# Attention and mixture of experts on one core: the tail rows' values as five wide float32 products, and four mixes moved ahead of five quarter operations

## The chip, the cores and the metric

The kernel runs on one core of a Trainium2 chip. The metric is the device time of one execution in microseconds (us), as the median of the runs shown. TensorE (PE) multiplies, VectorE (DVE), ScalarE (ACT) and GpSimd (POOL) work on tiles, and SyncE (SP) issues nearly all DMAs. Each engine takes its own instructions strictly in order and waits for the others by semaphores.

## The reference, cut to what matters

```python
def _attn_ref(q, k, v):                      # 2 x 8 heads x 576 rows x 64
    q_rot, k_rot = rotate(q), rotate(k)      # rotary embedding
    scores = scale * np.matmul(q_rot, k_rot.transpose(0, 1, 3, 2))
    scores = scores - np.max(scores, axis=-1, keepdims=True)
    attn = np.exp(scores)
    attn = attn / (np.sum(attn, axis=-1, keepdims=True) + 1e-09)
    return np.matmul(attn, v)

def _moe_ref(x, domain_probs, w1, w2):       # 1152 x 512, 4 experts, 1024 hidden
    p = domain_probs / (domain_probs.sum(-1, keepdims=True) + 1e-09)
    for e in range(E):
        h = np.maximum(x @ w1[e], 0.0)
        out += p[:, e:e + 1] * (h @ w2[e])

x = attn_out.transpose(0, 2, 1, 3).reshape(B * S, H * D)
return _moe_ref(x, **moe)
```

## The kernel before

**Attention.** Eight `Pair` objects, four head pairs for each of two batches, named 0_0 to 0_3 and 1_0 to 1_3. The 576 rows of a head are four row tiles of 128 and a tail of 64. A pair so has nine units: four row tiles of each head, and unit 8 (`TAIL`), which holds both heads' tails in one tile of 128 rows. For each unit TensorE makes the scores (`scores`), VectorE their maximum (`max`), ScalarE the exponentials and their row sum into column `u` of `total` (`exp`), TensorE turns the exponentials (`turn_e`, `turn_x`), and ScalarE and VectorE copy them out of PSUM in a high and a low part (`high`, `low`, `high_x`, `low_x`). Two units together make a product with V (`values`), whose two halves ScalarE and VectorE add (`lower`, `add`). These main rows are divided at the end: VectorE takes the reciprocals of `total` (`inverse`), spreads them (`spread`), TensorE turns them (`rows`), and VectorE multiplies (`divide`).

**The tail unit** goes another way. `scale` (L385) multiplies its exponentials by the reciprocals before `turn_e` turns them; `copy_e` and `copy_x` put the turned block into the tile `at` in float32; `tail_values` (L412) makes ten float32 products of 64 x 64, five for each head; `tail_high` and `tail_low` split the result, the second on VectorE.

**The order.** `Pair.place` (L432) puts every step at a due time in an agenda, from the tables `ALONE` (pairs of batch 0) and `BESIDE` (batch 1), and the program is emitted in that order. So each engine's queue is fixed by the tables. Rotations of later pairs run on GpSimd as jobs in between.

**The experts.** Rows are cut in chunk 0 (512 rows, class `Moe`) and chunk 1 (640 rows, class `Moe1`). Chunk 0 runs interleaved with the pairs of batch 1; its second layer's last results are weighted by `mix` (L605), one call per 128 rows. Chunk 1's first layer uses seven products of quarter matrices instead of eight. Sums of quarters of its input are made by `Quarters` (L624), three of four groups on GpSimd and the last, `second(nc.vector, 1)`, on VectorE. Its eight VectorE operations are `whole` and two `less`, `whole` and `less`, and three `low`. The sums of quarters of the weights are made by `Weights.sum` (L507), on GpSimd for the first block of the first expert and on VectorE for the others.

**PSUM.** The values' products of batch 0 share one bank, `xb[1]`, named x_113 before and x_114 after, in columns 256 to 511; the turned columns of keys 512 to 575 lie in `xb[0]`. From the end of batch 0 on only `xb[0]` is left for both.

```python
po = self.po = banks["x"].pick()[:, 2 * P : 2 * P + ST]
for j in range(2):
    for c in range(NS):
        n = P if c < NR else ST
        nc.tensor.matmul(po[j * D : (j + 1) * D, :], lhsT=self.raw["v"][0:n, j, c, :],
                         rhs=self.at[0:n, c, j * ST : (j + 1) * ST], start=(c == 0), stop=(c == NR))
```

Of the kernel before, what the change touches and what calls it, by code (L numbers as in the profile page):

```python
# [26 lines left out]
    copy_x=2.409, inverse=0.587, scale=0.712, spread=3.143, rows=4.075, divide=4.404, out_high=8.561,  # L27
    out_low=9.259, tail_values=4.354, tail_high=4.658, tail_low=4.771,
# [4 lines left out]
    tail_turn_x=1.122, copy_x=1.44, inverse=0.243, scale=0.697, spread=0.555, rows=2.195, divide=2.503,  # L33
    out_high=9.813, out_low=10.683, tail_values=2.033, tail_high=2.528, tail_low=2.554,
# [21 lines left out]
def kernel(  # L56
# [17 lines left out]
    nc = tc.nc  # L74
# [70 lines left out]
    class Pair:  # L145
# [9 lines left out]
        def load(self, s, queue=nc.sync, heads=((0, 2),)):  # L155

            hp, nm = self.hp, self.nm
            src = {"k": k, "q": q, "v": v}[s]
            x = self.pool.tile([P, 2, NS, D], F32, tag=f"raw{s}", name=f"raw{s}{nm}")
            hs = src[self.b, 2 * hp : 2 * hp + 2]  # L160
            for i, (a, z) in enumerate(heads):
                queue.dma_start(
                    out=x[:, a:z, 0:NR, :], in_=hs[a:z, 0:SM, :].rearrange("h (p r) d -> p h r d", r=NR)
                )
                if i:
                    continue
                for j in range(2):
                    rows = slice(j * ST, (j + 1) * ST)
                    if s == "v":
                        queue.dma_start(out=x[rows, :, NR, :], in_=hs[:, SM:S, :].rearrange("h p d -> p h d"))  # L170
                    else:
                        queue.dma_start(out=x[rows, 0, NR, :], in_=hs[j, SM:S, :])
# [29 lines left out]
        def split_v(self, eng_h=nc.gpsimd, eng_l=nc.gpsimd):  # L202
            self.vs = self.pool.tile([P, 2, NS, 2, D], F32R, tag="vs", name=f"vs{self.nm}")
            split(eng_h, eng_l, self.raw["v"], self.vs[:, :, :, 0, :], self.vs[:, :, :, 1, :])
# [105 lines left out]
        def turn_e(self, u):  # L310
# [6 lines left out]
            if u == TAIL:  # L317
                self.at = apool.tile([P, NS, P], F32, tag="at", name=f"at{nm}")
# [31 lines left out]
        def copy_e(self):  # L350
            nc.scalar.activation(out=self.at[:, 0:NR, :], in_=self.et.pop(TAIL), func=AF.Copy)

        def copy_x(self):
            nc.vector.tensor_copy(self.at[0:ST, NR, :], px[:, 0:P])
# [46 lines left out]

        def divide(self):
# [5 lines left out]
        def out_low(self):  # L408
            eng = nc.vector if (self.b, self.hp) == (B - 1, NP - 1) else nc.gpsimd
            eng.tensor_tensor(out=self.dst[1], in0=self.xf, in1=f32(self.dst[0]), op=ALU.subtract)  # L410

        def tail_values(self):  # L412
            po = self.po = banks["x"].pick()[:, 2 * P : 2 * P + ST]
            for j in range(2):
                for c in range(NS):
                    n = P if c < NR else ST
                    nc.tensor.matmul(  # L417
                        po[j * D : (j + 1) * D, :],
                        lhsT=self.raw["v"][0:n, j, c, :],
                        rhs=self.at[0:n, c, j * ST : (j + 1) * ST],  # L420
                        start=(c == 0),
                        stop=(c == NR),
                    )

        def tail_high(self):
            nc.scalar.activation(out=self.tail_dst[0], in_=self.po, func=AF.Copy)

        def tail_low(self):
            cH, cL = self.tail_dst
            nc.vector.tensor_tensor(out=cL, in0=self.po, in1=f32(cH), op=ALU.subtract)  # L430

        def place(self, u, t, step, o):  # L432
# [8 lines left out]
            if u == TAIL:  # L441
                at("tail_turn", self.turn_e, u)
                at("tail_turn_x", self.turn_x, u)
                for key in (
                    "copy_e", "copy_x", "inverse", "scale", "spread", "rows", "divide", "out_high", "out_low",
                    "tail_values", "tail_high", "tail_low",
# [676 lines left out]
```

## Time and profile before

| what | us |
|---|---|
| median of 3 runs | 574.27 |
| lowest and highest run | 572.32, 576.47 |
| the profiled execution, its own time | 573.63 |
| span of that execution, first to last instruction | 571.8 |

So 1.8 us lie around the span. The profile shows one execution. A matmul's duration there is its latency, and matmuls overlap: the pace of a row of them is the distance between their starts, or the time until the next instruction's start divided by their number. "PEld" is TensorE's weight load, which runs beside the matmuls. A row of a float32 product counts two instructions, so the ten products of a tail are "x20". The number in brackets is how long the engine had stood idle before the row, with the instruction that ended the wait.

### The profile page before, as it was taken

How to read it: one execution, taken by the hardware profiler on the slowest of the kernel's cores; microseconds unless marked ns; L12 is line 12 of the kernel's file. 1: busy time of each engine (PE TensorE's matmuls, PEld its weight loads, DVE VectorE, ACT ScalarE, POOL GpSimd, SP SyncE). 2: the span in 40 equal slices, each digit the busy share in tenths (PEclk: the TensorE clock that was granted, in tenths of full speed). 3: DMA queues.
4: the chain of work that ended last, by engine and by line, in shares of the span. 5: the costliest groups of instructions: out<-in, count | busy, mean ns of one | idle time of the engine just before them, and what ended most of it. 6: DMA issues, size and time to landing. Idle time of an engine off the chain costs nothing.

```text
span 571.8 us, 8611 instructions
## 1 busy us (share of the span) xinstructions
PE 545.8 (95%) x3229; PEld 478.5 (84%) x3229; DVE 325.4 (57%) x586; ACT 277.8 (49%) x545; POOL 337.5 (59%) x232
## 2 busy tenths in 40 slices
PE   4898988999999999999999998999999999999996
PEld 3788877888888888888888886998899899889985
DVE  5588898234362434444334435995578658757702
ACT  5678888365444544556436552554154225324500
POOL 7999965458824673379244388458663664565400
PEclk9999999899999999999999999999999999999999
DMA  5245023054224222442242222631323213223102
GB/s 151 70 115 136 18 56 97 18 172 153 73 62 156 73 75 54 121 120 70 76 104 79 66 75 76 222 107 38 109 78 100 65 57 111 75 73 78 72 0 92
DMA packets 42459, 50.67 MB, mean 89 GB/s; under 512 B 7218, under 2 KB 32050, under 8 KB 42418
## 3 DMA queue, kind: packets, MB, share of 16 engines
q1 hardware_dynamic: 41618, 49.38, 29.1%
q10 hardware_dynamic: 800, 0.75, 0.5%
q8 instruction: 25, 0.41, 0.3%
q14 instruction: 16, 0.13, 0.1%
HBM read 43.34 MB, written 2.36 MB: 80 GB/s over the span
## 4 chain that ended last, share of the span: by engine, by line
PE 78%; DVE 7%; ACT 7%; POOL 4%; issue 2%; DMA 1%; SPq 0%; ACTq 0%; POOLq 0%; DVEq 0%
PE po L824 6%; PE po L822 6%; PE po L823 6%; PE p L737 6%; PE p L739 5%; PE p L738 5%; PE sc L282 5%; PE ph L601 4%; PE ph L603 4%; PE ph L602 4%; PE po L578 4%; PE po L576 4%; PE po L577 4%; PE pp L315 4%; ACT e L301 3%; PE x L417 3%
## 5 line engine op out<-in xcount | busy, mean ns | idle before, releaser
L142 POOL TENSOR_TENSOR wl<-wr,wh 128x1024 fp32r<-128x1024 f32 x64 | 154.3, 2412 | 145.6 <-ACT wh L135 144.1
L135 ACT ACTIVATE wh<-wr 128x1024 fp32r<-128x1024 f32 x64 | 67.2, 1052 | 28.8 <-PE po L578 16.7
L293 DVE TENSOR_REDUCE mx<-sc 128x1 f32<-128x576 f32 x72 | 54.2, 752 | 37.7 <-PE sc L282 37.3
L301 ACT ACTIVATE e<-sc,mx 128x576 f32<-128x576 f32 x72 | 53.3, 740 | 22.1 <-DVE mx L293 21.6
L142 POOL TENSOR_TENSOR sl<-sf,sh 128x1024 fp32r<-128x1024 f32 x16 | 38.5, 2404 | 42.5 <-ACT sh L135 42.5
L824 PE MATMUL po<-wh,hL 128*128 128x512 f32 x160 | 62.3, 389 | 0.0
L823 PE MATMUL po<-wl,hH 128*128 128x512 f32 x160 | 62.3, 389 | 0.0
L822 PE MATMUL po<-wh,hH 128*128 128x512 f32 x160 | 62.3, 389 | 0.0
L562 DVE SCALAR_TENSOR_TENSOR hL<-ph,hH 128x512 fp32r<-128x512 f32 x32 | 22.1, 692 | 61.1 <-ACT hH L561 61.1
L576 PE MATMUL po<-wh,hH 128*128 128x512 f32 x128 | 52.3, 409 | 0.0
L601 PE MATMUL ph<-xH,wh 128*128 128x512 f32 x128 | 51.5, 402 | 0.0
L315 PE MATMUL pp<-ident,e 128*128 128x128 f32 x288 | 45.3, 281 | 5.9 <-DVE e L387 3.4
L332 ACT ACTIVATE ptH<-pp 128x512 fp32r<-128x512 f32 x64 | 38.1, 595 | 25.1 <-PE x L365 17.3
L578 PE MATMUL po<-wh,hL 128*128 128x512 f32 x128 | 50.3, 393 | 0.0
L336 DVE TENSOR_TENSOR ptL<-pp,ptH 128x512 fp32r<-128x512 f32 x64 | 43.9, 686 | 11.1 <-ACT ptH L332 10.8
L603 PE MATMUL ph<-xH,wl 128*128 128x512 f32 x128 | 50.1, 392 | 0.0
L577 PE MATMUL po<-wl,hH 128*128 128x512 f32 x128 | 50.0, 391 | 0.0
L602 PE MATMUL ph<-xL,wh 128*128 128x512 f32 x128 | 50.0, 391 | 0.0
L135 ACT ACTIVATE sh<-sf 128x1024 fp32r<-128x1024 f32 x16 | 16.9, 1059 | 67.1 <-DVE sf L516 67.1
L775 ACT ACTIVATE hH<-p 128x320 fp32r<-128x320 f32 x64 | 27.1, 435 | 40.3 <-DVE p L767 40.3
L315 PEld LDWEIGHTS pp<-ident,e 128*128 128x128 f32 x288 | 34.3, 143 | 12.2 <-issue 2.0
L516 DVE TENSOR_TENSOR sf<-wr 128x256 f32<-128x256 f32 x30 | 32.2, 1114 | 17.4 <-DMA wr<-in_moe_w_dram 17.4
(164 smaller groups left out, 1375.3 us busy)
## 6 DMA issues: line engine op xcount, KB each, us to landing
wr<-in_moe_w_dram SPq DMA_DIRECT2D x68, 512.0 KB, 3.6
k2T<-kT SPq DMA_DIRECT2D x14, 288.0 KB, 4.1
rawv<-in_v_dram SPq DMA_DIRECT2D x8, 256.0 KB, 3.1
out_dram<-acc SPq DMA_DIRECT2D x8, 256.0 KB, 2.5
rawk<-in_k_dram SPq DMA_DIRECT2D x7, 256.0 KB, 4.1
rawq<-in_q_dram SPq DMA_DIRECT2D x7, 256.0 KB, 3.0
rawv<-in_v_dram SPq DMA_DIRECT2D x16, 32.0 KB, 2.6
tabs<-in_rope_dram ACTq DMA_DIRECT2D x1, 320.0 KB, 3.5
```

Source lines behind the costliest of these rows:

```text
L135: nc.scalar.activation(out=hi, in_=src, func=AF.Copy)
L142: eng_l.tensor_tensor(out=lo, in0=src, in1=f32(hi), op=ALU.subtract)
L315: nc.tensor.transpose(pp[:, c * P : (c + 1) * P], self.e[u][:, c * P : (c + 1) * P], ident)
L576: nc.tensor.matmul(po[t], lhsT=sH, rhs=wH, start=(f == 0), stop=False)
L577: nc.tensor.matmul(po[t], lhsT=sH, rhs=wL, start=False, stop=False)
L578: nc.tensor.matmul(po[t], lhsT=sL, rhs=wH, start=False, stop=(f == NF - 1))
L601: nc.tensor.matmul(o, lhsT=wH[:, kt], rhs=xh, start=(kt == 0), stop=False)
L602: nc.tensor.matmul(o, lhsT=wH[:, kt], rhs=xl, start=False, stop=False)
L603: nc.tensor.matmul(o, lhsT=wL[:, kt], rhs=xh, start=False, stop=(kt == KT1 - 1))
L822: nc.tensor.matmul(po[t], lhsT=sH, rhs=wH, start=(f == 0), stop=False)
L823: nc.tensor.matmul(po[t], lhsT=sH, rhs=wL, start=False, stop=False)
L824: nc.tensor.matmul(po[t], lhsT=sL, rhs=wH, start=False, stop=(f == NF - 1))
```

## The change

- `scale` is gone. The exponentials of the tail are turned as they are.
- The transposed tail products have the reciprocals along the free axis. `tail_rows` turns `total`'s last column, broadcast to 128 columns, into 128 columns of PSUM; `keep_tail_rows` copies two blocks of 64 x 64 of them into the tile `xt` on ScalarE; `tail_divide` multiplies the two blocks of the product by them on VectorE.
- `tail_values` makes five products of 128 x 128: both heads' V side by side times all 128 tail columns. Only the two blocks of equal head are used. For that raw V is laid out with the heads inside, so its load is two DMAs of one head each, in rows of 256 bytes.
- The last 64 keys go into a constant tile `tail_keys`, whose lower half is set to zero at the start.
- `tail_low` reads `xt` and runs on GpSimd, except for the last pair.
- The swapped K of the very first pair (`lh`) takes the place of another tile.
- At the end of chunk 0, the four mixes now stand ahead of five of the eight quarter operations on VectorE.

```diff
 ALONE = dict(
-    copy_x=2.409, inverse=0.587, scale=0.712, spread=3.143, rows=4.075, divide=4.404, out_high=8.561,
+    out_low=9.259, tail_rows=1.6, keep_tail_rows=2.405, tail_values=4.354, tail_divide=4.658, tail_high=4.659, tail_low=4.771,
...
+            if s == "v":
+                x = self.pool.tile([P, NS, 2, D], F32, tag="rawv", name=f"rawv{nm}")
+                for j in range(2):
+                    queue.dma_start(out=x[:, 0:NR, j, :], in_=hs[j, 0:SM, :].rearrange("(p r) d -> p r d", r=NR))
+                for j in range(2):
+                    rows = slice(j * ST, (j + 1) * ST)
+                    queue.dma_start(out=x[rows, NR], in_=hs[:, SM:S, :].rearrange("h p d -> p h d"))
...
-            self.lh = apool.tile([P, NS, P], F32R, tag="at", name=f"lh{self.nm}")
+            self.lh = odds.tile([P, NS, P], F32R, tag="vs", name=f"lh{self.nm}")
...
-            nc.vector.tensor_copy(self.at[0:ST, NR, :], px[:, 0:P])
+            nc.vector.tensor_copy(tail_keys[0:ST], px[:, 0:P])
...
-        def scale(self):
-            e = self.e[TAIL]
-            nc.vector.tensor_scalar_mul(e, e, self.total[:, TAIL:])
...
+        def tail_rows(self):
+            self.prt = xb[1][:, 0:P] if banks["x"].n > 1 else xb[0][:, 3 * P : 4 * P]
+            nc.tensor.transpose(self.prt, self.total[:, TAIL:].to_broadcast([P, P]), ident)
+
+        def keep_tail_rows(self):
+            self.xt = apool.tile([P, ST], F32, tag="xt", name=f"xt{self.nm}", bufs=2)
+            for rows, cols in self.blocks():
+                nc.scalar.activation(out=self.xt[rows], in_=self.prt[rows, cols], func=AF.Copy)
+
+        def blocks(self):
+            return [(slice(j * D, (j + 1) * D), slice(j * ST, (j + 1) * ST)) for j in range(2)]
...
         def tail_values(self):
-            ...
+            po = self.po = banks["x"].pick()[:, 2 * P : 3 * P]
+            for c in range(NS):
+                nc.tensor.matmul(
+                    po,
+                    lhsT=self.raw["v"][:, c].rearrange("p h d -> p (h d)"),
+                    rhs=self.at[:, c, :] if c < NR else tail_keys,
+                    start=(c == 0),
+                    stop=(c == NR),
+                )
+
+        def tail_divide(self):
+            for rows, cols in self.blocks():
+                nc.vector.tensor_tensor(
+                    out=self.xt[rows], in0=self.po[rows, cols], in1=self.xt[rows], op=ALU.mult
+                )
 
         def tail_high(self):
-            nc.scalar.activation(out=self.tail_dst[0], in_=self.po, func=AF.Copy)
+            nc.scalar.activation(out=self.tail_dst[0], in_=self.xt, func=AF.Copy)
 
         def tail_low(self):
             cH, cL = self.tail_dst
-            nc.vector.tensor_tensor(out=cL, in0=self.po, in1=f32(cH), op=ALU.subtract)
+            self.spare_engine().tensor_tensor(out=cL, in0=self.xt, in1=f32(cH), op=ALU.subtract)
...
-    for x in qTt:
+    for x in (*qTt, tail_keys):
         nc.gpsimd.memset(f32(x), 0.0)
...
-    for i in range(6):
-        plan.at(end + last - 1.3 + 0.01 * i, quarter_step)
+    plan.at(end + last - 1.3, quarter_step)
...
         for x in moe0[0].mixes:
             moe0[0].mix(*x)
+        for _ in range(5):
+            quarter_step()
```

TensorE's queue at the tail of the first pair. `pp_0_8` is its turned tail, `sc_1_1` are scores of the next pair. Before:

```order
L315 MATMUL pp_0_8_544<-ident,e_0_8_513 128x128 x4
L282 MATMUL sc_1_1_565<-kT_1_415,qT_1_500 128x288 x2
L282 MATMUL sc_1_1_565<-k2T_1_427,qT_1_500 128x288 x2
L341 MATMUL x_112<-ident,e_0_8_513 64x128
L315 MATMUL pp_1_0_575<-ident,e_1_0_561 128x128 x4
```

And now:

```order
L322 MATMUL pp_0_8_547<-ident,e_0_8_517 128x128 x4
L407 MATMUL x_114<-ident,total_0_244 128x128
L289 MATMUL sc_1_1_569<-kT_1_419,qT_1_504 128x288 x2
L289 MATMUL sc_1_1_569<-k2T_1_431,qT_1_504 128x288 x2
L348 MATMUL x_113<-ident,e_0_8_517 64x128
L322 MATMUL pp_1_0_579<-ident,e_1_0_564 128x128 x4
```

The new row `x_114<-ident,total` stands between the turned tail and the next pair's scores, and it writes the bank that holds the values of the pair's third product.

ScalarE's queue at the same place, now (before, `at` was followed by `e_1_1` directly):

```order
L379 ACTIVATE tmp_0_2_557<-x_114 64x256
L308 ACTIVATE e_1_0_564,total_1_521<-sc_1_0_522,mx_1_0_553 128x576
L358 ACTIVATE at_0_8_552<-pp_0_8_547 128x512
L412 ACTIVATE xt_0_587<-x_114 64x64 x2
L308 ACTIVATE e_1_1_592,total_1_521<-sc_1_1_569,mx_1_1_577 128x576
```

The two copies into `xt` stand ahead of the exponentials of the next pair's second unit.

VectorE's queue at the end of chunk 0. `s` and `tL` are quarter operations, `acc` the mixes, `sf_1` weight sums of chunk 1. Before:

```order
L410 TENSOR_TENSOR xL_76<-xf_3_3536,xH_74 128x512
L644 TENSOR_TENSOR s_3926<-xH_74,xL_76 128x320
L649 TENSOR_TENSOR s_3863<-s_3926,s_3863 128x320
L649 TENSOR_TENSOR s_3926<-s_3926,s_3865 128x320
L644 TENSOR_TENSOR s_3932<-xH_74,xL_76 128x320
L649 TENSOR_TENSOR s_3932<-s_3932,s_3926 128x320
L660 TENSOR_TENSOR tL<-s_3863,tH 128x320
L660 TENSOR_TENSOR tL<-s_3926,tH 128x320
L660 TENSOR_TENSOR tL<-s_3932,tH 128x320
L611 SCALAR_TENSOR_TENSOR acc_0_1510<-po_3_0_3672,probs,acc_0_1510 128x512
L611 SCALAR_TENSOR_TENSOR acc_1_1511<-po_3_1_3673,probs,acc_1_1511 128x512
```

And now:

```order
L666 TENSOR_TENSOR s_3936<-xH_74,xL_76 128x320
L671 TENSOR_TENSOR s_3872<-s_3936,s_3872 128x320
L671 TENSOR_TENSOR s_3936<-s_3936,s_3874 128x320
L633 SCALAR_TENSOR_TENSOR acc_0_1517<-po_3_0_3682,probs,acc_0_1517 128x512
L633 SCALAR_TENSOR_TENSOR acc_1_1518<-po_3_1_3683,probs,acc_1_1518 128x512
L633 SCALAR_TENSOR_TENSOR acc_2_1519<-po_3_2_3684,probs,acc_2_1519 128x512
L633 SCALAR_TENSOR_TENSOR acc_3_1520<-po_3_3_3685,probs,acc_3_1520 128x512
L666 TENSOR_TENSOR s_3986<-xH_74,xL_76 128x320
L671 TENSOR_TENSOR s_3986<-s_3986,s_3936 128x320
L682 TENSOR_TENSOR tL<-s_3872,tH 128x320
L682 TENSOR_TENSOR tL<-s_3936,tH 128x320
L682 TENSOR_TENSOR tL<-s_3986,tH 128x320
```

The mixes have passed the last two sums and three `tL`; the same twelve operations stand ahead of `sf_1` in both.

## Rows read from the trace of the kernel before

**Rows 1.** The page, busy time of each engine in the span.

```profile
PE 545.8 (95%) x3229; PEld 478.5 (84%) x3229; DVE 325.4 (57%) x586; ACT 277.8 (49%) x545; POOL 337.5 (59%) x232
```

**Rows 2.** Windows: stretch, length, busy time of each engine (instructions), granted clock, DMA share, GB/s.

```profile
60.00:80.00 20.00, 18.19 (x153) 16.37 (x152) 16.91 (x30) 16.60 (x43) 19.26 (x18) 1.00 0.19 47
100.40:103.90 3.50, 3.50 (x22) 2.93 (x20) 1.16 (x3) 0.38 (x1) 0.00 (x0) 0.51 0.00 0
220.00:280.00 60.00, 60.00 (x348) 51.31 (x347) 25.63 (x44) 30.84 (x57) 33.65 (x22) 1.00 0.31 87
```

**Rows 3.** Waits: engine, line, what for: us in total, times, longest.

```profile
PE pp L315 <- DVE e L387: 3.4, 3, 1.8
PE p L737 <- DVE acc L611: 0.8, 1, 0.8
```

**Rows 4.** Lines: group, count, busy us, mean ns of one, idle before.

```profile
L315 PE MATMUL pp<-ident,e 128*128 128x128 f32 x288 | 45.3, 281 | 5.9 <-DVE e L387 3.4 <-DVE ptL L336 1.5 <-ACT e L301 0.9
L315 PEld LDWEIGHTS pp<-ident,e 128*128 128x128 f32 x288 | 34.3, 143 | 12.2 <-issue 2.0 <-ACT e L301 1.8 <-ACT tmp L372 1.6
L417 PE MATMUL x<-at,rawv 128*64 128x64 f32 (+1 forms) x160 | 15.0, 237 | 0.0
L387 DVE TENSOR_SCALAR e<-e,total 128x576 f32<-128x576 f32 x8 | 6.3, 788 | 0.1
L430 DVE TENSOR_TENSOR xL<-x,xH 128x64 fp32r<-128x64 f32 x8 | 1.8, 222 | 2.8 <-ACT xH L426 2.8
```

**Rows 5.** Timeline of the first pair's tail: start us, us, engine, line.

```profile
35.49 0.38 ACT L372 ACTIVATE tmp<-x 64x256 f32<-64x256 f32 x1 [0.22 <-PE x L368]
35.65 0.51 PE L282 MATMUL sc<-kT,qT 128*128 128x288 f32 x2
41.23 1.80 PE L417 MATMUL x<-at,rawv 128*64 128x64 f32 x20
42.95 0.66 PE L315 MATMUL pp<-ident,e 128*128 128x128 f32 x4
```

**Rows 6.** Timeline of the tail of pair 0_3, up to its tail products.

```profile
96.97 1.43 DVE L387 TENSOR_SCALAR e<-e,total 128x576 f32<-128x576 f32 x1
98.55 0.63 PE L315 MATMUL pp<-ident,e 128*128 128x128 f32 x4 [1.40 <-DVE e L387]
...
99.38 0.41 DVE L376 TENSOR_TENSOR xf<-x,tmp 64x256 f32<-64x256 f32 x1
...
99.84 0.39 PE L365 MATMUL x<-ptH,vs 128*128 128x256 f32 x1
...
102.42 2.38 PE L417 MATMUL x<-at,rawv 128*64 128x64 f32 x20
```

**Rows 7.** Timeline from the tail of pair 1_3 into chunk 1.

```profile
347.27 0.63 PE L315 MATMUL pp<-ident,e 128*128 128x128 f32 x4 [1.83 <-DVE e L387]
...
354.50 1.21 DVE L410 TENSOR_TENSOR xL<-xf,xH 128x512 fp32r<-128x512 f32 x1 [0.56 <-ACT xH L406]
...
358.47 1.03 DVE L644 TENSOR_TENSOR s<-xH,xL 128x320 f32<-128x320 f32 x1
...
361.14 2.72 DVE L611 SCALAR_TENSOR_TENSOR acc<-po,probs,acc 128x512 f32<-128x512 f32 x4
...
363.92 0.41 PE L737 MATMUL p<-xH,wh 128*128 128x320 f32 x1 [0.83 <-DVE acc L611]
...
376.18 0.48 DVE L777 SCALAR_TENSOR_TENSOR hL<-p,hH 128x320 fp32r<-128x320 f32 x1
...
377.21 0.31 PE L737 MATMUL p<-t1H,sh 128*128 128x320 f32 x1
```

**Rows 8.** The page's DMA issues: KB each, median us from issue to landing.

```profile
rawv<-in_v_dram SPq DMA_DIRECT2D x8, 256.0 KB, 3.1
...
rawv<-in_v_dram SPq DMA_DIRECT2D x16, 32.0 KB, 2.6
```

**Rows 9.** Timeline, the first reader of a loaded V.

```profile
10.52 0.77 ACT L135 ACTIVATE vs<-rawv 128x640 fp32r<-128x640 f32 x1
```

More of the change, by code (lines that the diff above doesn't have):

```diff
@@ L26 @@
     low_x=2.545, values=3.917, lower=4.47, add=4.785, tail_turn=1.096, copy_e=1.588, tail_turn_x=2.02,
-    copy_x=2.409, inverse=0.587, scale=0.712, spread=3.143, rows=4.075, divide=4.404, out_high=8.561,
-    out_low=9.259, tail_values=4.354, tail_high=4.658, tail_low=4.771,
+    copy_x=2.409, inverse=0.587, spread=3.143, rows=4.075, divide=4.404, out_high=8.561,
+    out_low=9.259, tail_rows=1.6, keep_tail_rows=2.405, tail_values=4.354, tail_divide=4.658, tail_high=4.659, tail_low=4.771,
 )
@@ L32 @@
     low_x=1.378, values=2.085, lower=2.576, add=2.643, tail_turn=1.093, copy_e=1.225,
-    tail_turn_x=1.122, copy_x=1.44, inverse=0.243, scale=0.697, spread=0.555, rows=2.195, divide=2.503,
-    out_high=9.813, out_low=10.683, tail_values=2.033, tail_high=2.528, tail_low=2.554,
+    tail_turn_x=1.122, copy_x=1.44, inverse=0.243, spread=0.555, rows=2.195, divide=2.503,
+    out_high=9.813, out_low=10.683, tail_rows=2.032, keep_tail_rows=2.1, tail_values=2.033, tail_divide=2.527, tail_high=2.528,
+    tail_low=2.554,
 )
@@ L167, in load @@
                 for j in range(2):
[L168 to L172, printed above, removed]
+                    queue.dma_start(out=x[j * ST : (j + 1) * ST, 0, NR, :], in_=hs[j, SM:S, :])
             self.raw[s] = x
@@ L350, in copy_e @@
         def copy_e(self):
[L351 removed]
+            nc.scalar.activation(out=self.at, in_=self.et.pop(TAIL), func=AF.Copy)
         def copy_x(self):
[L354 removed]
+            nc.vector.tensor_copy(tail_keys[0:ST], px[:, 0:P])
         def values(self, g):
@@ L408, in out_low, with spare_engine @@
         def out_low(self):
-            eng = nc.vector if (self.b, self.hp) == (B - 1, NP - 1) else nc.gpsimd
-            eng.tensor_tensor(out=self.dst[1], in0=self.xf, in1=f32(self.dst[0]), op=ALU.subtract)
+            self.spare_engine().tensor_tensor(out=self.dst[1], in0=self.xf, in1=f32(self.dst[0]), op=ALU.subtract)
         def tail_values(self):
[L413 to L423, printed above, removed]
+            po = self.po = banks["x"].pick()[:, 2 * P : 3 * P]
[12 more added lines that the diff above has]
+                )
         def tail_high(self):
-            nc.scalar.activation(out=self.tail_dst[0], in_=self.po, func=AF.Copy)
+            nc.scalar.activation(out=self.tail_dst[0], in_=self.xt, func=AF.Copy)
         def tail_low(self):
             cH, cL = self.tail_dst
-            nc.vector.tensor_tensor(out=cL, in0=self.po, in1=f32(cH), op=ALU.subtract)
+            self.spare_engine().tensor_tensor(out=cL, in0=self.xt, in1=f32(cH), op=ALU.subtract)
+        def spare_engine(self):
+            return nc.vector if (self.b, self.hp) == (B - 1, NP - 1) else nc.gpsimd
         def place(self, u, t, step, o):
@@ L444, in place @@
                 for key in (
-                    "copy_e", "copy_x", "inverse", "scale", "spread", "rows", "divide", "out_high", "out_low",
-                    "tail_values", "tail_high", "tail_low",
+                    "copy_e", "copy_x", "inverse", "spread", "rows", "divide", "out_high", "out_low", "tail_rows", "keep_tail_rows",
+                    "tail_values", "tail_divide", "tail_high", "tail_low",
                 ):
@@ L876 @@
     apool = attn.enter_context(tc.tile_pool(name="apool", bufs=1, side="right"))
+    tail_keys = apool.tile([P, P], F32, name="tail_keys")
     evens, odds = pools("pair")
```

9 lines of the change are left out of this document (6 added, 3 removed).

## The prediction

> **What bounds the kernel now.** Read the page's busy times first: PE is busy 545.8 of 571.8 us, the next engine, GpSimd, 337.5 [rows 1]. So 26 us of the span are not PE's, and a change pays in only two ways: by less work on PE, or by fewer of its waits. Then the windows, to see where PE is full. In 60 us of batch 1 it is busy for 60.00 [rows 2], so whatever leaves its queue there comes off the time at once. The list of waits tells which idle time the change can reach: 3.4 us in three waits of the turned tail for `scale` on DVE, and one wait of 0.83 us of chunk 1's products for the last mix [rows 3, 7]. The groups by line give prices: the tail products take 160 rows in all, 20 in each pair [rows 4]. Timelines come last, at the places where the order was changed.
>
> One line in the windows does not look like waiting, but is. From 100.40 to 103.90 PE is never idle, yet its granted clock is 0.51, the lower level of 1.2 GHz, where the stretches beside it have 1.00 [rows 2]. It follows the tail of pair 0_3, where PE had stood 1.40 us for `scale` [rows 6].
>
> **The tail products.** Before, 20 PE instructions of 64 columns go from 41.23 to the next start at 42.95: 1.72 us, or 0.086 each [rows 5]. Now there are 10 of 128 columns and one transpose of 128 columns. No such product is in the trace, so its price is bounded. The low end is the pace of the narrow ones, 0.086: the columns cost nothing. The high end takes the weight load as not hidden, 0.143 for a 128 x 128 float32 load [rows 4] in front of those 0.086: 0.23. The nearest row is the float32 transpose of 128 columns. Four of them span 0.63 us with the last one's latency, which is 0.281 in the mean, so (0.63 − 0.281) / 3 = 0.116 [rows 4, 6]. The latencies say something close: 281 ns at 128 columns less 237 at 64 is 0.044, and 0.086 + 0.044 = 0.13 [rows 4]. I take 0.115, since the transposes run at that pace with loads of the same size. Then a pair costs 10 x 0.115 + 0.115 = 1.27 instead of 1.72, which saves 0.46, or **3.7 us** in eight pairs. At the low end the gain is 8 x (1.72 − 0.98) = 6.0; at the high end there is a loss of 8 x (2.42 − 1.72) = 5.5. All eight pairs count in full, because PE is full around seven of them, and in pair 0_3 the products stand directly before the first expert's.
>
> **The waits for `scale`.** In pair 1_3 PE stands 1.83 us for it [rows 7]. The turned tail needs no division now, its exponentials are long there, and PE's next work is ready: **1.8 us**. In pair 0_3 the wait of 1.40 goes as well, but something else comes next. The third product's values started at 99.84, after the sum `xf` on DVE (99.38 + 0.41 = 99.79), because both use one bank [rows 6]. With the 1.43 us of `scale` out of DVE's queue, that sum ends about 1.4 earlier, at 98.4. But then the two copies into `xt`, which read the new columns in that bank, have to leave ScalarE first: 64 x 64 each, priced below the 0.38 that the 64 x 256 copy takes [rows 5], at about 0.25. That gives 99.0 as the new start, and a gain of **0.84**. In the third place the wait was 3.4 − 1.83 − 1.40 = 0.2, in pair 0_2. There I count **0.4**, that wait and as much again, since DVE's queue is shorter ahead of the values too. This is the least certain of the small terms.
>
> **The slow stretch.** 3.5 us at 0.51 do what would take about 1.75 at full clock [rows 2]. The tail products alone take 2.38 there against 1.80 [rows 5, 6]. The clock fell some 0.6 us behind the two stalls of that tail. The larger is removed and a stall of perhaps 0.8 us stays in front of the values, so the fall is more likely gone than not: **1.7 us**, else nothing.
>
> **The new handovers.** `tail_rows` writes the bank that ScalarE's `tmp` is still reading, so it cannot start before that copy ends. In the first pair the copy ends at 35.49 + 0.38 = 35.87, while the next pair's scores, which stand behind `tail_rows` in PE's queue, started at 35.65 [rows 5]. So about 0.2 is lost there, and as much or less in pair 0_1: **−0.3** in all. Behind the waiting transpose stand those scores, and behind them their maximum on DVE; neither has much slack this early. In batch 1 the transpose waits for the same sum `xf` that the products waited for before, and everything after it is on other engines: nothing.
>
> **What is hidden.** The copies into `xt` (under 0.8 us a pair on ScalarE, which is busy 49%), the zeroing of `tail_keys`, the new place of `lh` and `tail_low` on GpSimd cost nothing. GpSimd has 0.74 us left in 20 at its fullest [rows 2], but the waits show none of PE's for GpSimd behind the first stretch of the kernel; without that cover a `tail_low` of some 0.3 us would show in full. On DVE two `tail_divide`, each nearest to the 0.22 of `xL` [rows 4], replace one `scale` and one `tail_low`, so DVE becomes lighter in every pair but not at the one place where it is tight (below).
>
> V's load moves the same 256 KB in rows of 256 bytes and two DMAs. The tails' loads already go in such rows, and land in 2.6 us against 3.1 for the large one [rows 8]. The first V, issued at about 4.2, is read only at 10.52 [rows 9], so even a doubled landing of 6.2 would end near then: 0 by the rows, 0.4 at the worst.
>
> The Trainium skill, "DMA: Bandwidth & Descriptors", section Specifications, speaks against this edit: below 512 bytes a transfer does not reach line rate, because it turns into a read and a write-back. By it the time would come to 565.8 instead of 565.4. The trace's one case of such rows, the tails' load, is too small to show it either way.
>
> **The end of chunk 0.** The five quarter operations that the mixes pass took from 358.47 to 361.14, 2.67 us, so PE's wait of 0.83 for the last mix is gone [rows 7]. It is not free. The same twelve operations stand ahead of the weight sums, and for the last pair `tail_divide` and `tail_low` sit on DVE ahead of them, about +0.5 for the chain through `xL` at 354.50. DVE is then nearly the bound in chunk 1: the `hL` that ends at 376.18 + 0.48 = 376.66 frees a bank that PE wants at 377.21 [rows 7], a margin of 0.55. PE comes 0.83 earlier and DVE 0.5 later, so PE waits about 0.8 there. What the stall returns is taken again: **0**, with 0.8 to either side.
>
> **The sum.** 3.7 + 1.8 + 0.84 + 0.4 + 1.7 − 0.3 + 0 = 8.2. Against the profiled execution's 573.63, which is 571.8 of span and 1.8 around it, that is **565.4 us**. The median of the runs shown is 0.6 above that execution; the runs differ by more among themselves (572.3 to 576.5), so I add nothing.
>
> **Rivals.** *The slow stretch stays:* a stall of about 0.8 is left just before it, and the clock did fall behind stalls of 1.40 and 0.33. Against it, the stall is shorter. Without the 1.7: 567.1. *The wide products are no faster:* if the pace follows the columns fully, an instruction takes 0.172 and the products stay at 1.72, with the transpose on top. The first term turns from +3.7 to −0.9, and the time is 570.0. The transposes' 0.116 at 128 columns speaks against it. *DVE's backlog in chunk 1 is larger:* `tail_divide` has to wait for PE's product and ScalarE's copy, and each weight sum that comes late delays products. A loss of 1.5 gives 566.9. *Slower than before:* the loads of both heads' V are not hidden behind products of 128 columns, and an instruction costs 0.23. The products lose 5.5; of the 4.5 us of all other terms 2.8 stay, with the slow stretch kept: 573.63 + 5.5 − 2.8 = 576.3. It decides from the point where 8 x (10 w + 0.115 − 1.72) exceeds 2.8, at w = 0.196 us an instruction. PE's 0.086 with 64-column products, whose loads are hidden, speaks against it.
>
> **How the numbers follow.** Forecast 0.48, slow stretch 0.22, wide products no faster 0.15, backlog 0.10, slower 0.05. The range has its low end where the products reach 0.095 (8 x (1.72 − 1.06) = 5.3, or 1.6 more) and the boundary gives its 0.8 plus a little: 562.5. Its high end takes in the rival with no faster products, 570.0, with some of its small terms missed: 571.5. About 1%, 5.7 us here, is what a measurement of this kernel can tell from no change, so "faster" means below 568.5. Nearly all of the forecast (0.46), two thirds of the slow stretch's case (0.14) and some of the others (0.07) lie below: 0.67. Slower by over 1% needs more than the last rival's 576.3, so it has 0.03. The rest, 0.30, is within 1%.
>
> **What would show it.** In the changed profile the products should read "x10" with about 1.2 us from their start to the next instruction's; 1.7 or more makes the first term wrong. The waits for `scale` should be gone, with none over 0.4 of `tail_rows` for `tmp` or of the values for `xt` in batch 0. The window behind pair 0_3's tail should show a clock of 1.00, and PE's wait at the start of chunk 1 should turn up some 13 us later, as one for `hL`, or nowhere. The forecast is wrong if PE's busy time falls by less than 2 us, or if new waits of PE on DVE or ScalarE add up to more than 2 us.

## The result and the profile after

| | before | changed | ratio, 95% interval |
|---|---|---|---|
| first comparison, median | 573.62 us (4 runs) | 567.47 us (4 runs) | 0.9886 (0.9851 to 0.9921) |
| second comparison, median | 573.78 us (11 runs) | 567.71 us (6 runs) | 0.9903 (0.9877 to 0.9928) |
| the profiled execution | 573.63 us, span 571.8 | 566.62 us, span 564.8 | |

The change saves about 6 us, 1.0 to 1.1%, where 8.2 were forecast. The ten runs of the changed kernel lie between 566.4 and 569.6, so the profiled one is among the fastest; a second profile of it, from the second comparison, is of one of the slowest (569.33, span 567.5).

The lines below are from the first of the two. The busy times of the changed kernel's page answer to [rows 1]:

```profile
span 564.8 us, 8507 instructions
PE 539.7 (96%) x3157; PEld 474.3 (84%) x3157; DVE 324.0 (57%) x587; ACT 281.0 (50%) x561; POOL 339.3 (60%) x240
```

PE's busy time fell by 6.1 us, nearly all of the 7.0 by which the span fell. So its idle time hardly changed, 25.1 us after 26.0. The list of PE's waits says why (engine, line, what for: total, times, longest):

```profile
PE p L759 <- DVE hL L799: 1.3, 2, 0.8
...
PE sc L289 <- ACT kT L243: 0.7, 2, 0.4
...
PE x L372 <- ACT xt L412: 0.6, 1, 0.6
PE ph L624 <- POOL xL L424: 0.4, 1, 0.4
PE p L759 <- ACT p L766: 0.3, 1, 0.3
```

The 3.4 us for `scale` and the 0.8 for the last mix of [rows 3] are gone. In their place stand these, none of which the list of before has. Four of the five are for VectorE or ScalarE, 2.9 us together.

The tail of pair 0_3 on PE answers to [rows 6] (start, us, engine, line):

```profile
96.56 0.39 PE L372 MATMUL x<-ptH,vs 128*128 128x256 f32 x1 [0.57 <-ACT xt L412]
...
98.16 1.06 PE L430 MATMUL x<-at,rawv 128*128 128x128 f32 x8
99.05 0.39 PE L430 MATMUL x<-tail_keys,rawv 128*128 128x128 f32 x2
99.20 0.48 PE L623 MATMUL ph<-xH,wh 128*128 128x512 f32 x1
...
102.20 0.50 PE L624 MATMUL ph<-xL,wh 128*128 128x512 f32 x1 [0.43 <-POOL xL L424]
```

Ten wide products take 1.04 us (98.16 to 99.20). The start of chunk 1 answers to [rows 7]; PE first, from two stretches of its timeline, then VectorE:

```profile
364.38 0.42 PE L759 MATMUL p<-t1H,sh 128*128 128x320 f32 x1 [0.49 <-DVE hL L799]
369.84 0.41 PE L759 MATMUL p<-t1H,sh 128*128 128x320 f32 x1 [0.78 <-DVE hL L799]
```

```profile
345.36 1.27 DVE L449 TENSOR_TENSOR xL<-xt,xH 128x64 fp32r<-128x64 f32 x1 [0.32 <-ACT xH L445]
346.55 1.38 DVE L424 TENSOR_TENSOR xL<-xf,xH 128x512 fp32r<-128x512 f32 x1
...
350.81 2.73 DVE L633 SCALAR_TENSOR_TENSOR acc<-po,probs,acc 128x512 f32<-128x512 f32 x4
353.45 1.83 DVE L666 TENSOR_TENSOR s<-xH,xL 128x320 f32<-128x320 f32 x1
...
369.30 0.48 DVE L799 SCALAR_TENSOR_TENSOR hL<-p,hH 128x320 fp32r<-128x320 f32 x1
```

**Where the time went.** Take one PE instruction that both profiles have, and compare its start. The last column is what was gained since the row above it.

| PE instruction | before | after | difference | this stretch |
|---|---|---|---|---|
| turned last columns before the tail of 0_3 | 91.67 | 89.17 | −2.50 | −2.50: the tails of 0_0 to 0_2 |
| first value of the third product of 0_3 | 99.84 | 96.56 | −3.28 | −0.78: the wait of 1.40, less new waits |
| first product of the first expert | 104.74 | 99.20 | −5.54 | −2.26: products and slow stretch |
| fourth product that reads an `xL` there, the first of pair 0_3 | 107.16 | 102.20 | −4.96 | +0.58: wait for `xL` |
| `rows` of pair 1_2 | 291.81 | 285.05 | −6.76 | −1.80: three tails of batch 1 |
| turned tail of pair 1_3 | 347.27 | 338.46 | −8.81 | −2.05: the wait of 1.83 |
| `rows` of pair 1_3 | 352.42 | 342.99 | −9.43 | −0.62: its products |
| chunk 1, first product behind the mixes | 363.92 | 353.59 | −10.33 | −0.90: the wait for the mix |
| chunk 1, product of `t1H` of the second group | 377.21 | 369.84 | −7.37 | +2.96: waits for VectorE |
| the end of the span | 571.8 | 564.8 | −7.0 | +0.37 |

Up to 353.59 the gain has grown to 10.3 us; the forecast's terms add up to 9.0 there. Then 2.96 us are handed back within 16 us.

The second profile has the same table within 0.05 us in every stretch, but for two: the first is −0.25 instead of −2.50, and that of the tails of batch 1 is −1.30 instead of −1.80. Its end is 4.3 us ahead of before. Four kernels of the experiments have the same program as the changed one up to the first of these instructions, and start it at 90.47, 91.17, 91.24 and 91.45; the old program with the new order starts it at 91.15. So the −2.50 of the table is not shown to be the change's: five of six profiles of the new program lie at 90.47 or later, and the two of the old at 91.15 and 91.67.

### The profile page after: what moved, and what is told of

It reads as the page before. It is cut to its first block, busy times and chain, and to the rows that moved or that the text cites. A ratio compares the mean times of both kernels' runs of the same rounds, so it can differ in the third digit from the quotient of the medians.

```text
span 564.8 us, 8507 instructions
## 1 busy us (share of the span) xinstructions
PE 539.7 (96%) x3157; PEld 474.3 (84%) x3157; DVE 324.0 (57%) x587; ACT 281.0 (50%) x561; POOL 339.3 (60%) x240
## 5 line engine op out<-in xcount | busy, mean ns | idle before, releaser
L343 DVE TENSOR_TENSOR ptL<-pp,ptH 128x512 fp32r<-128x512 f32 x64 | 44.0, 687 | 11.1 <-ACT ptH L339 10.3
```

## The experiments

All times are medians, and the ratios are to the kernel before, run beside each kernel. The changed kernel stands at 0.9886 and 0.9903 in its two comparisons.

**1. The order of the mixes, apart from the tails.** Once the changed kernel with the old order, once the kernel before with the new one:

```diff
-    plan.at(end + last - 1.3, quarter_step)
+    for i in range(6):
+        plan.at(end + last - 1.3 + 0.01 * i, quarter_step)
...
-        for _ in range(5):
-            quarter_step()
```

> The changed kernel with the eight quarter operations ahead of the four mixes, as before the change. Theory (the mixes' place only moves a wait: VectorE has the same queue up to the first hL of chunk 1): TensorE waits 2.5 to 3.5 us for the last mix at the start of chunk 1, and in return its waits for hL (1.3 us in the changed kernel) and the 0.5 us of other small waits there vanish; 0 to 1 us slower than the changed kernel, 567.5 to 568.5. Rival (the new order itself made VectorE late): the waits for hL vanish and the wait for the mix is under 1.5 us, 1 to 3 us faster than the changed kernel, 564.5 to 566.5. Second rival (the order is worth the stall it removes and more): 2 to 3 us slower, 569.5 to 570.5.

> The kernel before with the four mixes ahead of five of the eight quarter operations, nothing else changed. Theory: the wait of 0.83 us for the last mix goes, and since TensorE then stands only 0.83 us earlier against VectorE, with a margin of 0.55 us at hL, about 0.3 us comes back as a wait for hL: 0.5 us faster than before, 572.5 to 573.5. Rival (the order costs by itself): waits for hL of over 1.5 us, 1 us slower, 574.5 to 575.

With the new order alone: 574.0 us, ratio 1.000 (0.9986 to 1.0014). Its waits for the mixes are gone, and PE waits for something else (list of waits):

```profile
PE p L737 <- DVE hL L777: 1.2, 2, 0.8
```

So the theory's mechanism holds, the wait moves on, but all of it came back: PE's product of `t1H` of the second group starts at 377.19, and at 377.21 in the kernel before. The rival, that the order costs by itself, is right in part. VectorE's rows say where, with GpSimd's last:

```profile
354.07 1.21 DVE L410 TENSOR_TENSOR xL<-xf,xH 128x512 fp32r<-128x512 f32 x1 [0.56 <-ACT xH L406]
...
360.67 1.97 DVE L644 TENSOR_TENSOR s<-xH,xL 128x320 f32<-128x320 f32 x1
...
364.29 0.75 DVE L516 TENSOR_TENSOR sf<-wr 128x256 f32<-128x256 f32 x2
```

```profile
359.88 2.42 POOL L142 TENSOR_TENSOR sl<-sf,sh 128x1024 fp32r<-128x1024 f32 x1 [1.17 <-ACT sh L135]
```

The sum that the mixes passed took 1.03 us at its old place [rows 7] and takes 1.97 here, beside GpSimd's `sl`. From `xL` to the first weight sum VectorE needs 10.22 us; before it needed 9.28, to the row

```profile
363.78 0.78 DVE L516 TENSOR_TENSOR sf<-wr 128x256 f32<-128x256 f32 x2
```

So the new order by itself makes VectorE 0.94 us later.

With the tails alone: 570.3 us, 0.9927 (0.9899 to 0.9955), some 1.4 to 2.4 us behind the changed kernel, though the intervals overlap. That is more than the theory's 0 to 1; the time itself is one that the second rival gave. In its profile the waits for `hL` are gone, and these stand there instead:

```profile
356.56 0.41 PE L759 MATMUL p<-xH,wh 128*128 128x320 f32 x1 [1.70 <-DVE acc L633]
358.53 0.64 PE L759 MATMUL p<-xH,wh 128*128 128x320 f32 x1 [0.83 <-DVE acc L633]
```

That is 2.5 us, as the theory had it. What it did not have is the clock behind them (window: length, busy PE, PEld, DVE, ACT, POOL, granted clock, DMA share, GB/s):

```profile
358.00:364.00 6.00, 5.47 (x20) 5.47 (x21) 4.45 (x11) 2.14 (x4) 2.78 (x2) 0.50 0.60 226
```

PE's lag behind the changed kernel grows from 4.9 us at the second wait to 7.1 at 363.2, at the lower level, 1.2 GHz. (2.3 of the lag were there before the waits, from the first stretch of the table.) Two of the eight runs took 567.0 and 567.4 us, as long as the changed kernel.

The granted clock of every run, in the mean over its span, is on record. With the tails alone it is 0.988 to 0.995 in the eight runs, 0.992 in the mean, and 0.995 and 0.993 in the two short ones; in the ten runs of the changed kernel it is 0.993 to 1.000, 0.998 in the mean. An estimate from these means: what the lower level costs, at half speed, is (1 − clock) x span, 4.5 us with the tails alone and 1.3 in the changed kernel. The 3.2 between them are more than the whole loss. So the order is worth nothing by itself, and the 1.4 to 2.4 us that it seems to be worth behind the new tails go with the clock. That the two waits bring it down was not tried.

**2. Narrow products, and V's load.** Ten products of 64 x 64 on the new layout, then these with V loaded by one DMA as before:

```diff
...
+            for j, (rows, cols) in enumerate(self.blocks()):
...
+                    nc.tensor.matmul(
+                        po[rows, cols],
+                        lhsT=self.raw["v"][0:n, c, j, :],
+                        rhs=self.at[0:n, c, cols] if c < NR else tail_keys[0:n, cols],
...
```

```diff
-                x = self.pool.tile([P, NS, 2, D], F32, tag="rawv", name=f"rawv{nm}")
+                x = self.pool.tile([P, 2, NS, D], F32, tag="rawv", name=f"rawv{nm}")
...
+                queue.dma_start(
+                    out=x[:, :, 0:NR, :], in_=hs[:, 0:SM, :].rearrange("h (p r) d -> p h r d", r=NR)
+                )
...
```

> The changed kernel with ten products of 64 x 64 a pair again, on the same layout of V, the division still behind them. Theory (TensorE bound; ten instructions of 128 columns take 1.04 us and twenty of 64 take 1.72): 8 x 0.68 = 5.4 us more TensorE time, of which up to 1.2 may vanish where a later wait swallows it (pairs 0_0, 0_1 and the last pair, behind which VectorE is late): 4.2 to 5.4 us slower than the changed kernel, 571.7 to 572.9. Rival (the width pays little, the rest of the change made the gain): under 2 us slower, below 569.5.

> The kernel with narrow products, with V laid out and loaded as before the change: one DMA in rows of 1 KB in place of two in rows of 256 bytes. Theory (the load is hidden in either form): the time of the narrow kernel, 571.4, within 0.5 us; the large load lands in about 3.1 us, no engine waits for V in either. Rival (a load in rows of 256 bytes comes late or slows others): 0.5 us or more faster than the narrow kernel, below 570.9, and the first split of V begins earlier.

Narrow: 571.38 us, 0.9966 (0.9950 to 0.9983), so the width is worth 0.6 to 0.8%, 3.6 to 4.6 us, around the theory's low end of 4.2. In batch 1 PE falls behind the changed kernel by 0.60, 0.76, 0.76 and 0.76 us at the four tails. The rival with under 2 us falls. With one load: 571.78, 0.9963 (0.9946 to 0.9981), no difference. The pages give the landing (KB each, median us), changed kernel first, then the one load:

```profile
rawv<-in_v_dram SPq DMA_DIRECT2D x16, 128.0 KB, 3.0
```

```profile
rawv<-in_v_dram SPq DMA_DIRECT2D x8, 256.0 KB, 2.8
```

Half the bytes in 256-byte rows land no sooner than the whole in rows of 1 KB, so such rows may well be slower per byte. But the first reader of V starts at 11.06 with one load and at 10.99 with two: the load is hidden in either form.

**3. The wait for `scale`, put back.**

```diff
+        def scale(self):
+            e = self.e[TAIL]
+            nc.vector.tensor_scalar_mul(e, e, 1.0)
...
```

The tables give it its old due times again.

> The changed kernel with the scale operation back at its old due times, multiplying the tail's exponentials by 1.0, so that the turned tail waits for it again. Theory: the waits of the turned tail for it come back with 1.8, 1.4 and 0.2 us, and some 0.5 us of other waits: 3.4 to 4.5 us slower than the changed kernel, 571 to 572; the stretch behind the tail of pair 0_3 shows the granted clock at 0.5 again and costs 1.7 us of this or on top of it. Rival (VectorE, late at the start of chunk 1, swallows the wait of pair 1_3): 1.5 to 2 us slower, 569 to 569.5. For the clock: if it does not fall behind a stall of 1.4 us there, the fall before was not that stall's.

572.4 us, 0.9978 (0.9961 to 0.9995): 0.75 to 0.92% or 4.3 to 5.3 us slower than the changed kernel, at or above the theory's end. The two long waits are back:

```profile
98.33 0.63 PE L322 MATMUL pp<-ident,e 128*128 128x128 f32 x4 [1.40 <-DVE e L407]
...
344.18 0.63 PE L322 MATMUL pp<-ident,e 128*128 128x128 f32 x4 [1.83 <-DVE e L407]
```

Against the changed kernel PE loses 1.58 and 1.99 us at them; 0.27 of the first is won back at the next products, and 1.0 of the second at the start of chunk 1. That leaves 2.3 us, in a traced run of 571.15. The rest is in part the clock: its mean is 0.992 to 0.997 in the ten runs, 0.995 in the mean, which by the estimate of experiment 1 costs about 1.6 us more than in the changed kernel. But it does not fall where the theory said: behind the wait of 1.40 us the clock stayed up (window as above):

```profile
98.00:104.00 6.00, 4.88 (x34) 4.30 (x35) 3.60 (x10) 1.81 (x6) 0.06 (x1) 1.00 0.01 3
```

**4. The new handovers.** First the other PSUM bank, then a later place:

```diff
-            self.prt = xb[1][:, 0:P] if banks["x"].n > 1 else xb[0][:, 3 * P : 4 * P]
+            self.prt = xb[0][:, 3 * P : 4 * P]
```

```diff
-    out_low=9.259, tail_rows=1.6, keep_tail_rows=2.405, tail_values=4.354, tail_divide=4.658, tail_high=4.659, tail_low=4.771,
+    out_low=9.259, tail_rows=4.353, keep_tail_rows=4.6, tail_values=4.354, tail_divide=4.658, tail_high=4.659, tail_low=4.771,
```

> The changed kernel with tail_rows writing the other PSUM bank, xb[0], in batch 0 too. Theory (the new handovers come from the shared bank): the values of pair 0_3 no longer wait 0.57 us for xt, and the transposes of pairs 0_0 to 0_2 no longer wait for tmp, 0.2 to 0.4 each: 0.5 to 1.3 us faster than the changed kernel, 566.2 to 567. Rival (the wait only changes banks, since the turned keys 512 to 575 lie in xb[0]): a wait of about the same size at the turned keys, within 0.3 us of the changed kernel.

> The changed kernel with tail_rows and its copies moved in batch 0 to directly before and behind the tail products, as in batch 1. Theory (the early place costs the waits for tmp and xt): the waits of 0.2 to 0.5 us at the tails of pairs 0_0 to 0_2 and the 0.57 us of pair 0_3's values go, 0.8 to 1.5 us faster than the changed kernel, 566 to 566.7. Rival (ScalarE, which then waits for the products with the next pair's turned keys behind it, gives it back): waits of the scores for kT grow by 0.3 us or more a pair, within 0.5 us or slower.

Other bank: 568.62 us, 0.9905 (0.9867 to 0.9942). The wait for `xt` is gone, and a larger one took its place, four times before the transpose itself:

```profile
PE x L407 <- DVE ptX L355: 2.1, 4, 0.9
```

Later place: 568.99 us, 0.9917 (0.9893 to 0.9941). The scores behind the first tail start 0.35 us sooner, which is lost again by the next turned exponentials; the wait for `xt` is gone, but these grow, from 0.7 and 0.4:

```profile
PE sc L289 <- ACT kT L243: 1.0, 2, 0.6
...
PE ph L624 <- POOL xL L424: 0.9, 1, 0.9
```

Neither theory's gain is there, and both rivals hold in kind: the handover found another partner in both places. The rivals' prices are not shown; the wait for `kT` grew by 0.3 us in all and not in each pair.

**5. The wait for `xL` at the first expert.**

```diff
-            return nc.vector if (self.b, self.hp) == (B - 1, NP - 1) else nc.gpsimd
+            return nc.vector if (self.b, self.hp) in ((0, NP - 1), (B - 1, NP - 1)) else nc.gpsimd
```

> The changed kernel with both low parts of pair 0_3 on VectorE instead of GpSimd. Theory (the first expert's products wait 0.43 us for GpSimd's 1.28 us operation behind ScalarE's high part; VectorE does it in 0.7 and stands idle there): the wait goes, 0.4 to 0.6 us faster, 566.9 to 567.1. Rival (ScalarE's high part, which stands behind the tail's own high part and so behind tail_divide, sets the time): the wait stays at 0.3 or more and the time within 0.2 us.

568.83 us, 0.9912 (0.9882 to 0.9942). In the trace the wait of 0.43 is gone, and PE's lag behind the changed kernel falls from 1.32 to 0.69 us there, by 0.63, as the theory had it. VectorE does the two operations in 0.23 and 0.69 us, beside an idle GpSimd:

```profile
101.61 0.23 DVE L449 TENSOR_TENSOR xL<-xt,xH 128x64 fp32r<-128x64 f32 x1 [0.32 <-ACT xH L445]
102.13 0.69 DVE L424 TENSOR_TENSOR xL<-xf,xH 128x512 fp32r<-128x512 f32 x1 [0.30 <-ACT xH L421]
```

The median does not show it: half a microsecond is less than the 2 us between runs.

**6. VectorE at the start of chunk 1.** The sum of weight block 1 on GpSimd, then the sums of blocks 1 to 3 left out:

```diff
-                (nc.vector if e or fb else nc.gpsimd).tensor_tensor(out=x[:, o], in0=p, in1=q, op=op)
+                (nc.vector if e or fb > 1 else nc.gpsimd).tensor_tensor(out=x[:, o], in0=p, in1=q, op=op)
```

```diff
+            if not e and fb:
+                nc.gpsimd.memset(x, 1.0)
-            for o, p, q, op in (
+            for o, p, q, op in () if not e and fb else (
```

> The changed kernel with the sum of the second weight block of chunk 1 on GpSimd, so that four operations of VectorE (1.6 us) leave its queue ahead of the first hL. Theory (VectorE's queue is the bound at the start of chunk 1 and gives back what the last pair's wait returned): the waits for hL of 0.5 and 0.8 us go, and some of the 1.2 us lost ahead of them; a new wait of up to 0.6 us for sl_1 may appear; 0.8 to 2.4 us faster than the changed kernel, 565.1 to 566.7. Rival (GpSimd, four times 1 us for the same sum, is late instead): TensorE waits over 1.5 us for sl_1 and the time is the same or up to 2 us longer.

> The changed kernel without VectorE's twelve operations for the sums of weight blocks 1 to 3 of chunk 1's first expert (GpSimd fills the tiles with ones instead, so that part of the computation is left out). Theory (VectorE's work is the bound there, with some 5.4 us a block against TensorE's 4.4): TensorE's waits for hL, 1.3 us, go, and most of the 3 us that it loses against the kernel before between 356 and 372 us: 2 to 3 us faster than the changed kernel, 564.5 to 565.5. Rival (the latency of the chain product, sum, high part, low part sets the pace, not the amount of work): the waits for hL stay above 1 us, under 0.7 us faster.

Sum on GpSimd: 568.06 us, 0.9902 (0.9878 to 0.9926), and the waits for `hL` are 1.3 us as before. By the rival GpSimd should have made PE wait; it did not. By the theory 1.6 us taken from VectorE should have helped; it did not either. VectorE's timeline shows where they went:

```profile
357.12 0.91 DVE L671 TENSOR_TENSOR s<-s,s 128x320 f32<-128x320 f32 x1
357.95 2.89 DVE L682 TENSOR_TENSOR tL<-s,tH 128x320 fp32r<-128x320 f32 x3
```

The same four operations take 0.49 and 1.29 us in the changed kernel, where GpSimd stands idle beside them. Here it computes the sum at that moment, and 2.0 us are lost for the 1.6 saved. So this run leaves the theory untested. The second one tests it, with a part of the computation left out: 565.35 us, 0.9851 (0.9819 to 0.9884), 2 to 3 us faster. The waits for `hL` are gone, and PE wins 0.34, 0.75 and 1.05 us between 362 and 370. What holds PE there is the amount of VectorE's work: in the changed kernel PE's second wait comes 369.84 − 364.38 = 5.46 us behind the first, a block of VectorE's work apart.

**7. All three put together, and the changed kernel once more.** `combined` is the later place of 4, the low parts of 5, and the tail's low part of pair 1_3 on GpSimd:

```diff
-            self.spare_engine().tensor_tensor(out=cL, in0=self.xt, in1=f32(cH), op=ALU.subtract)
+            (nc.gpsimd if self.b else self.spare_engine()).tensor_tensor(out=cL, in0=self.xt, in1=f32(cH), op=ALU.subtract)
```

> rows_late, with both low parts of pair 0_3 on VectorE, and the tail's low part of pair 1_3 on GpSimd. Theory: rows_late's gain, 0.5 us at the first expert, and VectorE's chain at the end of chunk 0 starts 0.7 us earlier, since the 64-column operation that took 1.27 us there leaves it: 1.5 to 2.5 us faster than the changed kernel, 565 to 566. Rival (VectorE's operations there are slowed by GpSimd's in any case, and what ScalarE waits for in batch 0 takes the rest): within 0.7 us of the changed kernel.

> The changed kernel as it is, beside the three others of this call. Both theories: 566.4 to 568.9 as in its first runs, median 567.5, 5.5 to 6.5 us below before; within one program, runs 2 us apart.

Combined: 568.7 us, 0.9913 (0.9889 to 0.9936), the rival. VectorE is rid of the 1.27 us, but its next sum then waits 0.21 us for GpSimd's result, a later one takes 2.69 us instead of 1.83 beside GpSimd's work, and PE waits 1.1 us for `p`. The changed kernel again: 567.71. No version tried that computes everything beats it.

## Why the forecast held, and where it did not

The forecast was 565.4, with terms that as printed add up to 8.1; the medians are 567.5 and 567.7, inside the range. That they are only 2 us off is in part luck: the terms were wrong by up to 2 us in both directions. One of the prediction's own signs of being wrong came true: new waits of PE on VectorE and ScalarE were to stay at 2 us or less and are 2.9. PE's busy time fell by 6.1, clear of the other sign's 2.

**The tail products: the right term, too small in batch 1 and too large in batch 0.** Forecast was a saving of 0.46 us a pair, 3.7 in all, at 0.115 us an instruction. Measured are 1.04 us for ten, or 0.104, at the tail of 0_3. From the tail products of pair 1_0 to those of 1_2 PE took 116.52 us before (173.56 to 290.08) and takes 115.17 in both profiles (168.76 to 283.93 in the first), 0.68 less a pair. Eight times that is 5.4; taking the width away again cost 3.6 to 4.6. That "all eight pairs count in full" is what does not hold: the first three, with 1.5 forecast for everything there, gave 0.2 to 1.2 in five of the six profiles named above. PE is not full in that stretch, 18.19 us of 20 [rows 2].

**The waits for `scale`: right.** 1.83 forecast for pair 1_3, 2.05 found. In pair 0_3 the values were to start 0.84 us earlier and limited by `xt`: they gained 0.78, and wait 0.57 for `xt`, more than the 0.4 that the prediction's signs allowed. The scores behind the first new transpose do start later, 0.71 us behind the turned tail instead of 0.35, but the transpose after them no longer waits for VectorE, and wins that back.

**The slow stretch: the right size, with an open cause.** Products and clock were to give 0.46 + 1.7 = 2.2 in front of the first expert; 2.26 were found, and the stretch from 98 to 104 has a granted clock of 1.00 (window):

```profile
98.00:104.00 6.00, 5.57 (x31) 4.49 (x30) 1.86 (x5) 2.18 (x5) 1.61 (x2) 1.00 0.00 0
```

But that the removed wait had brought it down there is not shown. With the wait of 1.40 put back the clock did not fall there (experiment 3), and the changed kernel's first profile has such a stretch elsewhere (last section). Over the runs, the mean clock of the kernel before is 0.995 to 0.996 in three groups of 11, 17 and 31 runs, and 0.998 in the ten of the changed one: by the estimate of experiment 1 some 1.0 to 1.5 us of the gain.

**The end of chunk 0: the term that failed most.** The step said that VectorE's chain through `xL` comes "about +0.5" late, so that the 0.83 us of the stall is taken back and the sum is 0, with 0.8 to either side. The mechanism was right to the place and the row: the wait for the mix went, and PE waits 0.78 us for the named `hL`. (That this equals the forecast 0.8 is luck: PE had already waited 0.49 us for the `hL` of the group before, and less for others.) Its formula holds as well: `hL` came 6.88 us earlier than before (376.18 to 369.30), PE's product 7.37, the margin of 0.55 being used up to 0.06. Only VectorE's lateness was mis-sized: PE stood 9.43 us earlier at `rows`, so it is 9.43 − 6.88 = 2.55 us instead of 0.5. The place cost 2.96 − 0.90 = 2.06 us net, as much as the gap between the 8.2 forecast and the 6 of the medians. In the second profile it cost the same, 2.06.

The lateness can be read off in three parts. From `rows` of pair 1_3 to the start of the long `xL` VectorE needed 2.08 us (352.42 to 354.50) and now needs 3.56 (342.99 to 346.55), 1.48 more. From there to the first weight sum it needed 9.28 and now needs 10.38, to

```profile
356.93 0.75 DVE L538 TENSOR_TENSOR sf<-wr 128x256 f32<-128x256 f32 x2
```

which is 1.10 more. From the weight sum to the named `hL` it is 12.40 and 12.37. The prediction had 0.5 for the first part and nothing for the second.

In the first part, `tail_low` was priced at the 0.22 us of [rows 4]; it took 1.27. The old one read PSUM and one tile in SBUF; the new one reads `xt` and `xH`, both in SBUF. Here are GpSimd's operations beside them, the kernel before and then the changed one:

```profile
351.93 2.39 POOL L142 TENSOR_TENSOR wl<-wr,wh 128x1024 fp32r<-128x1024 f32 x1 [2.31 <-ACT wh L135]
```

```profile
344.15 2.40 POOL L143 TENSOR_TENSOR wl<-wr,wh 128x1024 fp32r<-128x1024 f32 x1 [1.53 <-ACT wh L136]
...
352.54 2.39 POOL L143 TENSOR_TENSOR sl<-sf,sh 128x1024 fp32r<-128x1024 f32 x1 [1.17 <-ACT sh L136]
```

Before, the operation ran from 353.72 for 0.22 us in the middle of `wl`, undisturbed. Now it began at 345.36 and ended at 346.63, just behind GpSimd's end at 346.55. Where GpSimd does it (`combined`, experiment 7), the long `xL` starts 0.68 us sooner behind `rows`. The other 0.80 of the 1.48 is `tail_divide` with the handover to ScalarE ahead of `xL`.

The second part is mostly the quarter sum that the mixes passed. It was priced as unchanged; its new place is beside `sl` (352.54 to 354.93), and it takes 1.83 us instead of the 1.03 of [rows 7]. It does so with the old tail as well, in the kernel with the order alone (experiment 1). Wherever it starts, it ends 0.34 or 0.35 us behind the end of the GpSimd operation beside it: at 355.28 here behind 354.93, at 362.64 with the order alone behind 362.30, at 357.34 in `combined` behind 356.99. So its price here is what is left of GpSimd's operation, and 0.35.

The Trainium skill has the rule, which the prediction had not weighed: "SBUF — State Buffer", section "Who interferes with whom". An instruction of VectorE with two inputs in SBUF takes its second one through a read port that it shares with GpSimd's reads, and whichever began first keeps it to its end; with at most one input in SBUF, and outside VectorE's two-port modes, it is not touched. The trace agrees: 1.27 us against 0.22 beside the same kind of operation, and 0.23 in experiment 5 with GpSimd idle.

**A wait not foreseen.** PE waits 0.43 us (0.58 in the table) at the first expert. With `tail_divide` between the products and `tail_high`, ScalarE's high part of the main rows, queued behind `tail_high`, is late, and GpSimd's `xL` behind it. Experiment 5 takes it away.

**What was hidden stayed hidden:** V's load, as experiment 2 shows. The Trainium skill's rule on transfers below 512 bytes ("DMA: Bandwidth & Descriptors", section Specifications), by which the prediction had 0.4 us more, may be at work in the landing times, but it cost nothing that shows. For the copies into `xt` it holds only in part: they cost 0.57 us of PE's time in pair 0_3, which the forecast had counted there.

## What to carry to other kernels

Before an operand is moved from PSUM to SBUF to make an operation lighter, look at what GpSimd does at that moment: the price of a two-operand VectorE operation in the old trace holds only for the same operand places beside the same neighbour. And a wait that is removed directly ahead of a stage where another engine is nearly full pays only up to that engine's margin: work out the margin there first, as a row, and count every delay of that engine's chain against it. And of a stretch gained between two profiles, only what a second profile repeats is shown: here 2.25 of the first 2.50 us were not repeated.

## What the runs showed of the hardware

**Small VectorE operations take 0.17 or 1.4 us.** The scaling of nine columns of `total` in the second pair took, in the changed kernel's first profile and in its second:

```profile
53.95 0.17 DVE L389 TENSOR_SCALAR total<-total 128x9 f32<-128x9 f32 x1
```

```profile
55.89 1.40 DVE L389 TENSOR_SCALAR total<-total 128x9 f32<-128x9 f32 x1
```

The copy `rep` of the first pair took 0.55 and 1.46 us. GpSimd is nearly always busy in that stretch, 28.85 us of 30 from 30 to 60 in both. The two profiles are 2.3 us apart by 61 us, and the same from there to within 0.5. In the six profiles with the same program there, this operation took 0.17, 0.66 and four times 1.39 to 1.42 us, and PE started the first instruction of the table at 89.17, 90.47 and 91.17 to 91.45, in the same order. That such operations are the cause was not tried.

**Where the clock falls is not fixed by the wait ahead of it.** Seven profiles have one stretch of 3 to 7 us at the lower level before their last 10 us: 100 to 104 in the kernel before, 99 to 103 with the order alone, 18 to 21 in the changed kernel, 19 to 23 with `scale` kept, 17 to 25 in the two with narrow products, 358 to 364 with the tails alone. The other seven, the second of the changed kernel among them, have none there. The changed kernel's stretch, as a window:

```profile
18.00:21.00 3.00, 2.44 (x11) 2.37 (x12) 1.07 (x2) 1.59 (x5) 2.92 (x4) 0.50 0.37 104
```

At 22.3 us that profile is 0.8 us ahead of the second one, which had 1.00 throughout, so in that place the stretch cost nothing that shows. What decides between the places is open.
